# Attention plus MLP on one core: tails ahead of the main transposes, masks of batch 1 on VectorE, w_out sums one chunk later, casts ahead of loads

## The chip, the core and the metric

The kernel runs on one core of a Trainium2 chip. The core has TensorE (PE in the profile, with its weight loads as PEld), VectorE (DVE), ScalarE (ACT), GpSimd (POOL) and the queues that issue DMA transfers, of which SP and POOL matter here. The metric is the device time of one execution in microseconds (us).

## The reference

Input: q, k, v of 8 batches, 8 heads, 576 positions, 64 elements each; a two-layer MLP with w_in 512x2048, w_out 2048x512 and a slope alpha per hidden unit. All is float32 outside.

```python
scores = scale * np.matmul(q, k.transpose(0, 1, 3, 2))
mask_local = (rel >= 0) & (rel < 32)                  # heads 0 to 3
mask_strided = (rel >= 0) & (pos[None] % 32 == pos[:, None] % 32)   # heads 4 to 7
attn = softmax(np.where(masks, scores, -1e9))
x = (attn @ v), put as 4608 tokens x 512
h = x @ w_in
out = (np.maximum(h, 0) + alpha * np.minimum(h, 0)) @ w_out
```

Here rel is the query position less the key position.

## The kernel before

The work is in 16-bit floats with 32-bit sums. A batch has two **units** of four heads: the local heads (unit 2b) and the strided ones (unit 2b+1); a unit has two **pairs** of heads, so there are 32 pairs. For a unit, `transpose_piece` (L234) transposes q and then k on TensorE, eight 128x128 blocks each, into a PSUM tile `tp`, and copies them to SBUF (`qT`, `kT`). The rows 512 to 575 of q and k, loaded apart as a tile `tl`, are the **tails**: `tails` (L268) transposes them into a tile `tt`, and copies q's part on VectorE and k's part on ScalarE. For batches 0 and 1 (`early`) the two halves of each main copy are shared between VectorE and ScalarE (L256 to L262), and `tails` is called between k's two halves. One half of the copies waits for the other, since both read one PSUM tile. The tiles `tp`, `tt`, `pv`, `xp` and some scores share a ring of three PSUM banks (pool `ps`).

For a pair, scores are made in two groups (et tiles), exponentiated by ScalarE, and masked. Then `pv_piece` (L435) multiplies by v on TensorE (v has a column of ones, which gives the row sums), and VectorE takes the reciprocal (L458) and multiplies (L460). `x_piece` (L465) or a DMA transpose puts the result into `xT`.

There are three forms of masking. Batch 0 uses `score_piece` (L330), which adds a large negative mask (`madd`) to the scores by a matmul with the identity, ahead of the exponential. Batch 1 uses `score_early` (L290): it makes both score groups of a pair, adds the masks by four matmuls of 288 columns (L320), and then calls the exponentials (L323, L327). From batch 2 on, `score_both` (L388) masks after the exponential, by a multiplication with 0 or 1 on GpSimd (L423, L430).

The MLP goes over 9 chunks of 512 tokens. Layer 1 of a chunk is 16 `lin1_piece` (L623) of four matmuls; ScalarE makes the negative part (L643) and VectorE joins it (L646). Layer 2 of chunks 0 and 1 is 16 `lin2_piece` (L652) of four matmuls of 512 columns; from chunk 2 on, `lin2_sums` (L719) uses seven products of sums of blocks instead of eight products. It needs sums of blocks of w_out, which `w_sums` (L680) makes once: sums 1, 2 and 4 during layer 2 of chunk 0, and sum 3 in chunk 2.

The order is written out by hand: every instruction stays on its engine in program order (`keep`). Attention work is cut into pieces (L494 to L601), and `attn_step` (L611) runs the next piece between pieces of the MLP. The head (L864 to L882) runs batch 0's pieces with a few warming matmuls (`warm`) between them. Then come layer 1 of chunk 0 without attention pieces, and layer 2 of chunk 0 with batch 1's pieces, in the order that `alone(3, 2)` (L513) gives: q and k of the strided unit, scores of its two pairs, then pv pieces mixed with the transposes and scores of the local unit, and at last the x pieces. The first pieces of batch 2 follow.

GpSimd's queue carries loads that it issues itself and casts. Between L890 and L902 stand, in this order: the loads of batch 2's local q and k, two casts of batch 1's strided v (`cast_v`), the cast of batch 1's local q (`cast_l`), batch 2's tail loads, the cast of local k, a copy inside v (`over_v`), and more loads and casts for batch 2. The k and q casts feed the transposes of batch 1's local unit.

Of the kernel before, what the change touches and what calls it, by code (L numbers as in the profile page):

```python
# [11 lines left out]
ALU = mybir.AluOpType  # L12
AF = mybir.ActivationFunctionType
# [18 lines left out]
def kernel(  # L32
# [10 lines left out]
    nc = tc.nc  # L43
    keep = tc.keep_in_program_order
# [4 lines left out]
    SCALE = 1.0 / float(np.sqrt(D))  # L49
# [144 lines left out]
    def cast_v(b, pr, eng):  # L194

        v16 = vss[b % 2]
        cast_copy(eng, v16[0:72, 2 * pr : 2 * pr + 2, :, 0:64],
                  loaded[b][0:72, 1024 * pr : 1024 * pr + 1024].rearrange(
                      "p (h t d) -> p h t d", h=2, t=8))
        cast16[(b, True, "v")] = v16  # L200
# [33 lines left out]
    def transpose_piece(u, nm):  # L234

        b, strided = u // 2, u % 2 == 1  # L240
        early = b < NEARLY
        src = cast16[(b, strided, nm)]
        dst = qTs[u % 2][:, :, 0:576] if nm == "q" else kTs[u % 2][:, :, 32:608]
        tp = pspool.tile([128, 8, 64, 2], F16, tag="ps", name="tp")
        for j in range(8):
            blk = (src[:, j % 2, 128 * (j // 2) : 128 * (j // 2) + 128] if strided
                   else src[:, j].rearrange("p f d -> p (f d)"))
            keep(nc.tensor.transpose(tp[:, j].rearrange("r p e -> r (p e)"), blk, ident))  # L248
        if strided:
            main = tp.rearrange("r j p e -> r e j p")  # L250
            o = dst.rearrange("r e (j p) -> r e j p", j=8)[:, :, :, 0:64]
        else:
            main = tp.rearrange("r t p e -> r e p t")
            o = dst[:, :, 0:512].rearrange("r e (p t) -> r e p t", t=8)
        if early:
            for e in range(2):  # L256
                eng = "dve" if (nm == "q") == (e == 0) else "act"
                if u == 0 and nm == "q":
                    eng = "dve"
                if nm == "k" and e == 1:  # L260
                    tails(b, u, strided)
                cast_copy(eng, o[:, e : e + 1], main[:, e : e + 1])  # L262
            return
        cast_copy("act", o, main)
        if nm == "k":
            tails(b, u, strided)
# [23 lines left out]
    def score_early(P):  # L290

        w, r = P.w, 72 if P.strided else 128
        todo = []
        for i in range(2):
            et = ets[ectr["i"] % NE]
            ectr["i"] += 1
            if i:
                sps = [hbank() for _ in range(2)]
            else:
                sp = pbpool.tile([128, 2, 512], F32, tag="sp", name="sp")  # L300
                sps = [sp[:, y] for y in range(2)]
            grp = P.sgroups[i]
            n = w * len(grp)
            for x, t in enumerate(grp):
                k0 = 32 + 72 * t if P.strided else 96 * t
                for y in range(2):
                    hf = slice(64 * y, 64 * y + 64)
                    keep(nc.tensor.matmul(
                        sps[y][:, w * x : w * x + w], P.kT[hf, k0 : k0 + 128],
                        P.qT[hf, w * t : w * t + w], start=(x == 0), stop=False, skip_group_check=True))  # L310
                    P.et[(2 * (t // 2) + y, t % 2) if P.strided else (t, y)] = (et, n * y + w * x)
            todo.append((i, et[0:r, 0 : 2 * n], sps, n))
        for i, ev, sps, n in todo:
            if not P.strided and i == 0:
                m = madd[:, 0:288]
            else:
                m = madd[0:72, 288:360] if P.strided else madd[:, 96:192]
                m = m.unsqueeze(1).to_broadcast([r, n // w, w])
            for y in range(2):
                keep(nc.tensor.matmul(  # L320
                    sps[y][:, 0:n], ident[0:r, :], m, start=False, stop=True, skip_group_check=True))
            if i == 0:
                keep(nc.scalar.activation(  # L323
                    ev.rearrange("r (y c) -> r y c", y=2), sp[0:r, :, 0:n], AF.Exp, scale=SCALE))
                continue
            for y in range(2):
                keep(nc.scalar.activation(  # L327
                    ev[:, n * y : n * y + n], sps[y][0:r, 0:n], AF.Exp, scale=SCALE))

    def score_piece(P, i):  # L330

# [101 lines left out]
            defer.extend([lambda: ex(0), lambda: ex(1)])  # L433

    def pv_piece(P, a):  # L435
        while defer and any(P.et[z][0] is defer_et["et"] for z in P.et):
            defer.pop(0)()
        if P.x16 is None:
            if P.xd and P.strided:
                P.x16 = x16s  # L440
            else:
                P.x16 = xpool.tile([128, 1024], F16, tag="x16", name="x16")
        v16 = cast16[(P.b, P.strided, "v")]
        grp = P.pgroups[a]
        r = 72 if P.strided else 128
        pv = pspool.tile([128, 512], F32, tag="ps", name="pv")
        nb = 2 * len(grp)
        for x in range(nb):
            t, hh = grp[x // 2], x % 2
            et, c = P.et[(t, hh)]  # L450
            keep(nc.tensor.matmul(  # L451
                pv[:, 65 * x : 65 * x + 65], et[0:r, c : c + 128],
                v16[0:r, 2 * P.pr + hh, t, :] if P.strided else v16[:, 6 * (2 * P.pr + hh) + t, :],
                start=(x == 0), stop=(x == nb - 1), skip_group_check=True))
        w = P.w
        rc = rpool.tile([128, 8], F32, tag="rc", name="rc")
        pvv = pv[0:w, 0 : 65 * nb].rearrange("r (c e) -> r c e", e=65)
        keep(nc.vector.reciprocal(rc[0:w, 0:nb], pvv[:, :, 64]))  # L458
        c0 = 128 * grp[0]
        keep(nc.vector.tensor_tensor(  # L460
            P.x16[0:w, c0 : c0 + 64 * nb].rearrange("r (c e) -> r c e", e=64),
            pvv[:, :, 0:64],
            rc[0:w, 0:nb].unsqueeze(2).to_broadcast([w, nb, 64]), op=ALU.mult))
# [75 lines left out]
    for g in range(7, npair + 2):  # L539
        c = g // 4  # L540
# [68 lines left out]
    late = []  # L609

    def attn_step(end):  # L611
        if pos["i"] < end:
            pieces[pos["i"]][1]()
            pos["i"] += 1
        while late:
            late.pop(0)()
        if defer:
            defer.pop(0)()
# [188 lines left out]
    def warm(n):  # L807

        for _ in range(n):
            keep(nc.tensor.matmul(wps, wrm[:, 0:128], wrm, start=True, stop=True))  # L810
# [58 lines left out]
        madd, consts[:, 128:488], -1.0, 30000.0, op0=ALU.add, op1=ALU.mult))  # L869
    apt = pspool.tile([128, 512], F32, tag="ps", name="apt")  # L870
    for i in range(end0):
        if i == 9:
            keep(nc.tensor.transpose(apt[:, 0:16], alpha_r, id16))
            keep(nc.vector.tensor_scalar(
                oma, apt[:, 0:16], -1.0, 1.0, op0=ALU.mult, op1=ALU.add))
        if i == 8:
            cast_v(0, 0, "dve")
        attn_step(end0)
        if i < 2:
            warm(4)  # L880
        elif i > 8 and i not in (10, 13, 15):
            warm(1)  # L882

    def attn_n(n, end):
        for _ in range(n):
            attn_step(end)
        if n == 0:
            attn_step(0)

    load_qk(2, False, "q")  # L890
    load_qk(2, False, "k")
    for pr in range(2):
        cast_v(1, pr, "pool")
    cast_l(1, "q")
    load_tail(2, False)
    cast_l(1, "k")
    over_v(1, "pool")
    load_v(2, False)
    load_d(2)
# [8 lines left out]
        attn_n(0, end1)  # L908
    for i in range(16):
        lin2_piece(0, i)  # L910
        if i in (1, 3, 5):
            w_sums(nc.vector, ({1: 1, 3: 2, 5: 4}[i],))
        attn_n((0, 1, 1, 1, 1, 2, 1, 2, 1, 2, 1, 2, 2, 3, 2, 0)[i], end1)
        if i > 13:
            attn_n(1, end1 + 2)
# [5 lines left out]
    for n in range(1, NCH):  # L921
        ab = attn_until(n + 1) if n + 1 < B else len(pieces)
        left = ab - pos["i"]
        acc = 0.0
        for i in range(32 if n == 1 else 30):
            if i < 16:
                if n > 1:
                    lin1_piece(n, 8 * (i % 2) + i // 2)
                    if i in (5, 9, 13):
                        g_sum(nc.gpsimd, n, 1, i // 2 - 2, i // 2)  # L930
                else:
                    lin1_piece(n, i)
            elif n == 1:
                lin2_piece(n, i - 16)
            else:
                lin2_sums(n, i - 16)
                if n == 2 and i == 20:
                    w_sums(nc.vector, (3,))
            acc += left / (22.5 if n == 1 else 19 if n == B - 2 else 20.5) * (0.5 if i < 16 else 1.0)
            cnt = int(acc)  # L940
            acc -= cnt
            attn_n(cnt, ab)
        while pos["i"] < ab:
            attn_step(ab)
# [30 lines left out]
```

## Time and profile before

| | us |
|---|---|
| median of 6 runs | 311.62 (310.78 to 312.41) |
| the profiled execution | 311.78 |
| its span, first to last instruction | 310.0 |

| stage of the profiled execution | from | to | TensorE busy | VectorE busy | GpSimd busy |
|---|---|---|---|---|---|
| head: batch 0's attention | 0 | 23.0 | 23.00 | 15.99 | 18.41 |
| layer 1, chunk 0 | 23.0 | 38.5 | 15.38 | 12.23 | 4.16 |
| layer 1, chunk 1 | 62.6 | 78.7 | 16.06 | 12.30 | 9.23 |
| the rest, from chunk 2 on | 96.9 | 310.0 | 207.48 | 157.06 | 101.08 |

The two stages left out, layer 2 of chunks 0 and 1, are shown word for word in the prediction. The busy time of TensorE in the head has the warming matmuls in it. Times are from the start of the span. In a timeline a row has the start, the time, the engine, the line, the operation, the output and input tiles, the shape and a count; in square brackets stands the idle time ahead of it with what ended it. Rows of one engine may overlap by about 0.1 us. For a matmul the time includes the way through the array: four matmuls of 512 columns show 1.03 us, while the next matmul starts 0.86 us after the first. The granted TensorE clock was 0.999 of full speed.

### The profile page before, as it was taken

What the parts mean: (1) busy time and instruction counts of PE and PEld (TensorE: products, weight loads), DVE (VectorE), ACT (ScalarE), POOL (GpSimd) and SP (SyncE); (2) the same over time, 40 slices, a digit from 0 to 9 for tenths busy, and PEclk for the clock granted to TensorE, in tenths of its full rate; (3) what the DMA queues carried; (4) which work ended last, traced back from release to release, by engine and by line L of the source; (5) the groups of instructions that cost most, each with busy time, mean ns of one, the idle gap of its engine ahead of it and who ended that gap; (6) DMA issues with size and microseconds to landing.
All of it is one profiled execution on the core that took longest, in us unless ns stands there. A gap on an engine that the chain in (4) does not pass through costs nothing.

```text
span 310.0 us, 7066 instructions
## 1 busy us (share of the span) xinstructions
PE 300.3 (97%) x2803; PEld 192.5 (62%) x2803; DVE 219.2 (71%) x409; ACT 177.9 (57%) x330; POOL 170.0 (55%) x176
## 2 busy tenths in 40 slices
PE   8899989999999999999999999999999999999995
PEld 3554455654554468645888887448844784685484
DVE  6687875558533988488748874887579958855872
ACT  3656653597547764677467665766476336515630
POOL 8772399747979764967396719671825302201200
PEclk9999999999999999999999999999999999999999
DMA  7999999999899984999499819972911040012003
GB/s 233 195 207 206 213 205 199 174 170 257 145 172 220 154 102 38 152 271 128 61 174 261 100 30 181 142 82 37 190 53 22 2 123 34 2 51 87 0 3 135
DMA packets 81201, 40.38 MB, mean 130 GB/s; under 512 B 58624, under 2 KB 76304, under 8 KB 81168
## 3 DMA queue, kind: packets, MB, share of 16 engines
q0 software_dynamic: 41728, 17.38, 48.2%
q1 hardware_dynamic: 39168, 22.03, 32.3%
q10 hardware_dynamic: 272, 0.52, 0.5%
q8 instruction: 22, 0.36, 0.5%
q14 instruction: 11, 0.09, 0.1%
HBM read 38.01 MB, written 9.44 MB: 153 GB/s over the span
## 4 chain that ended last, share of the span: by engine, by line
PE 67%; DVE 12%; ACT 7%; POOL 4%; issue 4%; DMA 4%; SPq 0%; ACTq 0%; POOLq 0%; DVEq 0%
PE hb L633 27%; PE hb L752 20%; PE hb L660 6%; DVE gT L646 5%; DMA kl<-in_k_dram 4%; PE pv L451 3%; DVE x L460 2%; PE tp L248 2%; POOL vs L192 2%; ACT neg L643 2%; ACT et L421 2%; ACT xT L490 2%; PE sp L408 2%; ACT et L427 1%; PE xp L468 1%
## 5 line engine op out<-in xcount | busy, mean ns | idle before, releaser
L633 PE MATMUL hb<-xT,win 128*128 128x512 f16 (+1 forms) x640 | 132.9, 358 | 0.7
L646 DVE SCALAR_TENSOR_TENSOR gT<-neg,oma,hb 128x512 f16<-128x512 f32 x144 | 105.1, 744 | 38.3 <-ACT neg L643 31.9
L643 ACT ACTIVATE neg<-hb 128x512 f32<-128x512 f32 x144 | 86.0, 597 | 38.7 <-PE hb L633 37.3
L633 PEld LDWEIGHTS <-win 128*128 128x128 f16 x640 | 60.0, 98 | 56.6 <-issue 2.9
L423 POOL TENSOR_TENSOR et<-et,consts 128x576 f16<-128x576 f16 (+1 forms) x24 | 30.6, 1276 | 52.1 <-ACT et L421 52.1
L704 POOL TENSOR_TENSOR gsum<-gT 128x512 f16<-128x512 f16 x21 | 24.2, 1150 | 50.6 <-DVE gT L646 50.6
L752 PEld LDWEIGHTS <-gsum 128*128 128x128 f16 x448 | 41.3, 97 | 5.9 <-DVE gsum L704 1.1
L752 PEld LDWEIGHTS <-gT 128*128 128x128 f16 x336 | 31.4, 98 | 6.7 <-DVE gT L646 1.6
L460 DVE TENSOR_TENSOR x<-pv,rc 96x384 f16<-96x384 f32 (+2 forms) x62 | 33.0, 532 | 2.1
L660 PE MATMUL hb<-wout,gT 128*128 128x512 f16 x128 | 32.3, 379 | 0.0
L430 POOL TENSOR_TENSOR et<-et,consts 128x576 f16<-128x576 f16 (+1 forms) x24 | 30.6, 1277 | 0.6 <-ACT et L427 0.6
L764 ACT COPY o<-hb 128x512 f32<-128x512 f32 (+1 forms) x28 | 15.8, 565 | 26.4 <-PE hb L752 26.4
L451 PEld LDWEIGHTS <-et 72*128 72x128 f16 (+1 forms) x448 | 23.6, 98 | 9.6 <-DVE vs L190 0.4
L752 PE MATMUL hb<-wout,gT 128*128 128x256 f16 x216 | 28.0, 273 | 0.5
L458 DVE RECIPROCAL rc<-pv 72x6 f32<-72x6 f32 (+2 forms) x80 | 14.6, 183 | 19.5 <-PE pv L451 19.5
L752 PE MATMUL hb<-wout,gsum 128*128 128x256 f16 x216 | 26.9, 273 | 0.2 <-DVE gsum L704 0.2
L752 PE MATMUL hb<-wsum,gsum 128*128 128x256 f16 x216 | 26.3, 273 | 0.2 <-DVE gsum L704 0.2
L421 ACT ACTIVATE et<-sp 128x576 f16<-128x576 f32 (+1 forms) x24 | 15.5, 645 | 17.9 <-PE sp L408 17.9
L767 DVE TENSOR_TENSOR o<-hb,o 128x512 f32<-128x512 f32 (+1 forms) x21 | 14.2, 677 | 14.3 <-PE hb L752 10.6
L427 ACT ACTIVATE et<-sph 128x288 f16<-128x288 f32 (+1 forms) x48 | 18.2, 409 | 0.0
L192 POOL COPY vs<-stv 72x1024 f16<-72x1024 f16 x15 | 17.2, 1154 | 0.0
L660 PEld LDWEIGHTS <-gT 128*128 128x128 f16 x128 | 10.9, 97 | 9.0
(105 smaller groups left out, 324.2 us busy)
## 6 DMA issues: line engine op xcount, KB each, us to landing
out_dram<-o SPq DMA_DIRECT2D x27, 256.0 KB, 3.0
kl<-in_k_dram SPq DMA_DIRECT2D x6, 512.0 KB, 7.9
ql<-in_q_dram SPq DMA_DIRECT2D x5, 512.0 KB, 7.5
stv<-in_v_dram POOLq DMA_DIRECT2D x8, 288.0 KB, 7.5
vl<-in_v_dram POOLq DMA_DIRECT2D x6, 384.0 KB, 8.7
win<-in_moe_w_in_dram POOLq DMA_DIRECT2D x4, 512.0 KB, 11.7
wout<-in_moe_w_out_dram POOLq DMA_DIRECT2D x4, 512.0 KB, 14.2
out_dram<-osb SPq DMA_DIRECT2D x8, 256.0 KB, 5.6
```

The source lines that it names most:

```text
L192: keep(nc.gpsimd.tensor_copy(o, i))
L421: keep(nc.scalar.activation(ev.rearrange("r (y c) -> r y c", y=2), sp[0:r, :, 0:n], AF.Exp, scale=SCALE))
L423: keep(nc.gpsimd.tensor_tensor(mv, mv, m, op=ALU.mult))
L430: keep(nc.gpsimd.tensor_tensor(mv, mv, m, op=ALU.mult))
L451: keep(nc.tensor.matmul(pv[:, 65 * x : 65 * x + 65], et[0:r, c : c + 128], v16[0:r, 2 * P.pr + hh, t, :] if P.strided else v16[:, 6 * (2 * ...
L460: keep(nc.vector.tensor_tensor(P.x16[0:w, c0 : c0 + 64 * nb].rearrange("r (c e) -> r c e", e=64), pvv[:, :, 0:64], rc[0:w, 0:nb].unsqueeze ...
L633: keep(nc.tensor.matmul(hps[:, dst : dst + w], win16[:, kk, 128 * m : 128 * m + 128], xT[:, kk, src : src + w], start=(kk == 0 and x == 0) ...
L643: keep(nc.scalar.activation(neg, hps, AF.Relu, scale=-1.0))
L646: keep(nc.vector.scalar_tensor_tensor(gTs[n][:, m, :], neg, oma[:, m : m + 1], hps, op0=ALU.mult, op1=ALU.add))
L660: keep(nc.tensor.matmul(ops, gTs[n][:, kf, 128 * mt : 128 * mt + 128], wout16[:, kf, :], start=(kf == 0), stop=(kf == 15)))
L704: keep(eng.tensor_tensor(o[:, k0:k1], x[:, k0:k1], y[:, k0:k1], op=op))
L752: keep(nc.tensor.matmul(dst, lhs[:, kf, 128 * mt : 128 * mt + 128], rhs[:, kf, :], start=(first and own and kf == 0), stop=(kf == 7), skip ...
```

## The change

1. **Tails first.** For batches 0 and 1, `tails` is called ahead of k's main transposes, not between the two copies of k. So the `tt` bank is taken ahead of k's `tp` bank, and the small copies stand ahead of k's main copies on ScalarE and VectorE.
2. **Masks of batch 1 on VectorE.** `score_early` loses its 16 mask matmuls. After the exponentials it puts a multiplication of the et tile with the 0/1 mask on a list; `run_masks`, called at the start of each `attn_step` and each `pv_piece`, gives it to VectorE two steps later or when its pair's pv piece comes.
3. **w_out sums 1, 2 and 4** move from layer 2 of chunk 0 (after its pieces 1, 3 and 5) to layer 2 of chunk 1 (after its pieces 2, 6 and 10). They stay on VectorE.
4. **GpSimd's queue.** The four casts of batch 1 (v, q, v, k in this order) stand ahead of the loads of batch 2's q and k and of its tails.
5. In the head, the transpose of alpha and the scaling that reads it go from step 9 to step 3, and one warming matmul goes.

```diff
@@ transpose_piece
+        if early and nm == "k":
+            tails(b, u, strided)
         tp = pspool.tile([128, 8, 64, 2], F16, tag="ps", name="tp")
...
-                if nm == "k" and e == 1:
-                    tails(b, u, strided)
                 cast_copy(eng, o[:, e : e + 1], main[:, e : e + 1])
@@ score_early
-                        P.qT[hf, w * t : w * t + w], start=(x == 0), stop=False, skip_group_check=True))
+                        P.qT[hf, w * t : w * t + w], start=(x == 0), stop=(x == len(grp) - 1),
+                        skip_group_check=True))
...
-            for y in range(2):
-                keep(nc.tensor.matmul(
-                    sps[y][:, 0:n], ident[0:r, :], m, start=False, stop=True, skip_group_check=True))
...
+            if not P.strided and i == 0:
+                mv = ev.rearrange("r (y c) -> r y c", y=2)
+                m = mfirst.unsqueeze(1).to_broadcast([r, 2, n])
+            else:
+                mv = ev.rearrange("r (c f) -> r c f", f=w)
+                m = (mstr if P.strided else mother).unsqueeze(1).to_broadcast([r, 2 * n // w, w])
+            dmask.append([0, P, lambda mv=mv, m=m: keep(
+                nc.vector.tensor_tensor(mv, mv, m, op=ALU.mult))])
+
+    dmask = []
+
+    def run_masks(P=None):
+
+        for z in list(dmask):
+            z[0] += P is None
+            if z[0] > 1 or z[1] is P:
+                z[2]()
+                dmask.remove(z)
@@ pv_piece
+        run_masks(P)
@@ attn_step
+        run_masks()
@@ the head
-        if i == 9:
+        if i == 3:
             keep(nc.tensor.transpose(apt[:, 0:16], alpha_r, id16))
...
-            warm(4)
+            warm(4 - i)
@@ GpSimd's queue
+    cast_v(1, 0, "pool")
+    cast_l(1, "q")
+    cast_v(1, 1, "pool")
+    cast_l(1, "k")
     load_qk(2, False, "q")
     load_qk(2, False, "k")
-    for pr in range(2):
-        cast_v(1, pr, "pool")
-    cast_l(1, "q")
     load_tail(2, False)
-    cast_l(1, "k")
     over_v(1, "pool")
@@ layer 2 of chunk 0
-        if i in (1, 3, 5):
-            w_sums(nc.vector, ({1: 1, 3: 2, 5: 4}[i],))
@@ layer 2 of chunk 1
+                if i in (18, 22, 26):
+                    w_sums(nc.vector, ({18: 1, 22: 2, 26: 4}[i],))
```

More of the change, by code (lines that the diff above doesn't have):

```diff
@@ L313, in score_early @@
         for i, ev, sps, n in todo:
[L314 to L318, printed above, removed]
-            for y in range(2):
-                keep(nc.tensor.matmul(
-                    sps[y][:, 0:n], ident[0:r, :], m, start=False, stop=True, skip_group_check=True))
             if i == 0:
@@ L324, in score_early @@
                     ev.rearrange("r (y c) -> r y c", y=2), sp[0:r, :, 0:n], AF.Exp, scale=SCALE))
[L325 to L328, printed above, removed]
+            else:
+                for y in range(2):
+                    keep(nc.scalar.activation(
+                        ev[:, n * y : n * y + n], sps[y][0:r, 0:n], AF.Exp, scale=SCALE))
+            if not P.strided and i == 0:
+                mv = ev.rearrange("r (y c) -> r y c", y=2)
+                m = mfirst.unsqueeze(1).to_broadcast([r, 2, n])
+            else:
+                mv = ev.rearrange("r (c f) -> r c f", f=w)
[9 more added lines that the diff above has]
+                dmask.remove(z)
     def score_piece(P, i):
```

## The prediction

> **What bounds the kernel now.** I read the page's engine totals first, then a table of engine time by stage, then the chain of waits inside the one stage where TensorE stands still, and last the timelines of the instructions that the change touches.
>
> ```profile
> PE 300.3 (97%) x2803; PEld 192.5 (62%) x2803; DVE 219.2 (71%) x409; ACT 177.9 (57%) x330; POOL 170.0 (55%) x176
> ```
> ```profile
> 38.50:62.60 24.10, 22.66 (x271) 13.94 (x269) 14.62 (x31) 12.39 (x27) 20.97 (x22) 1.00 1.48 194
> 78.70:96.90 18.20, 18.04 (x174) 9.38 (x171) 7.02 (x19) 9.96 (x19) 16.13 (x17) 1.00 0.95 154
> ```
> TensorE (first busy column of the table) sets the end: it is busy 97% of the span and 18.04 of 18.20 us in layer 2 of chunk 1. The stage with a hole is layer 2 of chunk 0 (38.50 to 62.60), where it is busy 22.66 of 24.10 and GpSimd (fifth column) 20.97. So an edit counts where it takes matmuls away or closes that hole. The chain inside this stage:
>
> ```profile
> 38.33 1.22 DVE wsum L692
> ...
> 40.70 0.72 POOL ql L123
> ...
> 42.18 3.81 POOL vs L192 x2
> 45.99 0.99 POOL ql L192
> ...
> 47.03 0.62 PE tp L248 x8
> ```
> GpSimd issues batch 2's loads, makes two v casts and only then batch 1's q cast; the transposes of q on TensorE wait for it until 47.03 (1.21 us of TensorE idle in the waits). The v casts took 3.81 us for two, where one alone takes 1.03.
>
> ```profile
> 42.14 0.42 PE L320 MATMUL sp<-madd,consts 72*128 72x288 f16 x2
> 42.39 0.41 PE L320 MATMUL hb<-madd,consts 72*128 72x288 f16 x2
> 42.64 0.60 PE L660 MATMUL hb<-wout,gT 128*128 128x512 f16 x2
> ```
> The four mask matmuls of one score_early occupy TensorE from 42.14 to 42.64, 0.50 us. Two of VectorE's w_out sums (3.19 us from 41.90) run beside the slow casts.
>
> **The head, to 22.7 us: a loss.** Tails before the main transposes change the order on ScalarE. The rows of batch 0's second unit, ScalarE's and then VectorE's (start, us, engine, line):
>
> ```profile
> 12.56 0.57 ACT L188 COPY kT<-tp 128x512 f16<-128x512 f16 x1
> 13.03 0.27 ACT L188 COPY kT<-tt 128x128 f16<-128x128 f16 x1
> ```
> ```profile
> 12.63 0.21 DVE L190 COPY qT<-tt 128x128 f16<-128x128 f16 x1
> 13.16 0.69 DVE L190 COPY kT<-tp 128x512 f16<-128x512 f16 x1 [0.32 <-ACT kT L188]
> 13.77 0.48 DVE L190 COPY vs<-stv 72x1024 f16<-72x1024 f16 x1
> ```
> The first pv piece starts at 14.31, after 0.32 of waiting for that last copy. Today ScalarE's main copy of k starts at 12.56. In the new order it stands behind ScalarE's tail copy, which by the built program's waits needs VectorE's tail copy of q, and that stands behind two q copies. Steps: (1) batch 0's first unit: ScalarE has the same qT copy and kT copy, but both small tail copies ahead instead of one of them; the first scores start at about 9.84, not 9.70 (+0.14). (2) The alpha transpose now stands between the two score pieces; its row is 0.23, I take 0.15 since matmuls overlap. (3) q copies then end at 13.0 instead of 12.72, VectorE's tail copy at 13.12, ScalarE's tail copy at 13.42 and, with 0.1 overlap as in the rows, its main copy at 13.90 instead of 13.13. VectorE's second half, the v cast and the first pv follow: +0.77. From there VectorE runs reciprocal and multiply (0.19 and 0.55) ten times almost without a gap until 22.33, so nothing absorbs it. The sum is 0.77; it cannot be a gain, because no copy leaves this path, so the bounds are 0 and 1.0 (0.77 plus the rest of the 0.23). One warming matmul less (0.22) falls into an idle wait: nothing. The scaling that reads alpha (0.16 on VectorE) falls between its waits: nothing.
>
> **Layer 2 of chunk 0: the gain**, walked on before's clock. A layer-2 step is 0.86 on TensorE, a transposed unit 0.45.
> (a) No w_out sum stands ahead of the first q copy, and the tails come first: the first score_early starts at 41.60 instead of 41.77. Its masks go, 0.50. The second one must still wait for exponentials to free its banks, as now. Its masks go, 0.50.
> (b) On GpSimd the first v cast starts at 40.70, when the load issue ahead of it ends. Its data landed at 40.15 (issue 29.35 plus 10.8) and q's at 41.48. With nothing from VectorE beside them the casts take 1.03, 1.04, 1.03 and 1.07: q is ready at 42.8. TensorE comes to it at 44.50 and ends it at 44.95, now 47.48: **2.53 gained**, the hole included.
> (c) What is late next: the q copies of this unit. VectorE's queue is now reciprocal and multiply (to 45.47), two masks, q's first half (0.68), and then ScalarE's half (0.58), which frees the bank that the k transposes now use. (Before, the tails used it.) I price a mask by the same kind of instruction of nearly its size:
>
> ```profile
> 114.12 0.43 DVE L704 TENSOR_TENSOR gsum<-gT 128x512 f16<-128x512 f16 x1
> 114.47 1.29 DVE L704 TENSOR_TENSOR gsum<-gsum,gT 128x1024 f16<-128x1024 f16 x2
> ```
> 512 elements 0.43, 1024 elements 0.68 each: 576 elements 0.46, and 0.85 for a pair with their overlap. The bank is free at 47.55, TensorE is there at 46.97: 0.58 lost, gain 1.95. The bounds of a mask are 0.43 and 1.35 (the same 128x512 form at 240.96, beside GpSimd work); I take 0.46, since most masks meet GpSimd while it issues loads.
> (d) Two more score_early lose 0.50 each: 2.95.
> (e) At the end, masks of both last pairs (1.7 us) stand between reciprocals and multiplies; the last pv piece and the last x transposes wait about 0.4 together: **2.55**.
>
> Three edges of this. The last v copy of the unit still waits for its landing at 48.3, and ends a little earlier than now. Batch 2's q and k loads go out 4.2 us later (44.95 instead of 40.70); with 8.6 us they land at 53.6, their casts end by 56, and TensorE wants them from about 58. If that cover of 2 us went, each us more would count in full. The tail loads behind them only move with GpSimd's queue, the SP queue keeps its order, and transposed loads shift with TensorE.
>
> A row speaks on contention: beside two w_out sums (3.19) two v casts cost 1.75 more than 2 times 1.03. The Trainium skill, GPSIMD Engine Reference, Specifications, says that GpSimd's SBUF interfaces are shared with VectorE and contend with instructions that have two SBUF inputs. The masks are of that kind and the matmuls were not, so the rule speaks against this edit. By it each mask would hold GpSimd for its own length, eight by 0.46 or 3.7 us, the batch-2 casts would end near the 58 us where they are wanted, and up to 1 us of the gain would go; by the row beside load issues nothing goes.
>
> **W_out sums in chunk 1.** Three by 1.21 on VectorE, which is busy 7.02 of 18.20 us there and waits 0.21 to 1.75 before each reciprocal. They delay the reciprocal by 0 to 1.0 (by their places); the bank that it frees is wanted 2 us later. GpSimd loses up to 1.0 per sum (2.03 against 1.03) and has 2.07 idle; its masks are made about 2 us ahead of pv. I take nothing; the bounds are 0 and 1.73 each (1.94, the slower of the two sums shown, less the smallest wait of 0.21). It cannot gain: nothing leaves that stage.
>
> **Sum.** 0.77 minus 2.55 is -1.78. The profiled execution took 311.78 (span 310.0 and 1.8 around it), which gives 310.0; the median of the runs is 311.62, 0.16 lower, so 309.8.
>
> **Rivals.** *VectorE becomes the bound* in layer 2 of chunk 0. For it: a mask beside GpSimd can take 1.35, and masks stand ahead of copies that TensorE wants. Against: the VectorE time is no larger than the sums that leave (eight by 0.46, 3.7, against 4.41). At 0.9 per mask, between the two rows, the waits of (c) and (e) grow by some 0.9 each, the gain falls to about 0.8 and the head eats it: 311.5. *The head costs nothing*, if ScalarE's small copies fall into waits; against it are the dependencies above. Then 309.1. *Slower:* the w_out sums in chunk 1 hold the banks of pv and GpSimd's masks. For it: that stage has no hole on TensorE and GpSimd is 89% busy. Against: the waits of VectorE quoted. It decides once TensorE loses over 0.9 per sum (1.78 plus 0.93, by three); two of three at their bound of 1.73 cost 3.5: 313.3. *Not doing what it says*, q still late, is unlikely: its data landed at 41.48, three us before TensorE comes.
>
> **Numbers.** Forecast 0.48 (309.4 to 310.7 by itself: the head's upper bound, and masks up to 0.65 whose waits cost 0.4 twice), head free 0.17, VectorE bound 0.20, slower 0.15. 0.3% is 0.93 us, about what this measurement tells from none. So faster 0.65, same 0.20, slower 0.15. The range leaves out the slow case and reaches past the VectorE case and below the free head: 308.8 to 312.0.
>
> **What would show it.** Right: no mask matmuls, masks near 0.46 on VectorE; q's transposes at about 45.3 (44.5 plus the head) without a wait for GpSimd; the first layer-1 matmul near 23.5; chunk 1's first transposes at about 58.8 instead of 60.6; a TensorE wait for ScalarE's q copy before k's transposes. Wrong: first layer-1 matmul at 22.75 or before (head free), masks over 0.8, or TensorE waiting in 78 to 97.

## The result, and the profile after

The changed kernel took 310.29 us in the median of 25 runs; the kernel before took 311.57 in 53 runs beside it. The ratio, taken over the fast runs alone (one of the 25 was slow), is 0.9966 [0.9957, 0.9976], so the change makes the kernel faster by 0.34%. The forecast of 309.8 was 0.5 us too low; 310.29 lies inside the 309.4 to 310.7 that the prediction gave to its own mechanism. The profiled execution took 311.04 (span 309.2).

The totals of the page, and the two layer-2 stages of the table by stage (from:to, length, then busy time of PE, PEld, DVE, ACT, POOL, granted clock, DMA share, GB/s):

```profile
PE 297.7 (96%) x2786; PEld 190.9 (62%) x2786; DVE 222.9 (72%) x417; ACT 178.3 (58%) x330; POOL 169.7 (55%) x176
```
```profile
38.50:60.00 21.50, 20.00 (x241) 11.61 (x240) 15.34 (x38) 10.88 (x26) 19.19 (x22) 1.00 1.45 199
76.50:95.00 18.50, 18.33 (x177) 9.67 (x176) 11.79 (x25) 9.91 (x18) 15.47 (x15) 1.00 0.90 171
```

TensorE lost 2.6 us of work (297.7 against 300.3), yet the span shrank by 0.8. In layer 2 of chunk 0 there is still a hole: 20.00 busy of 21.50. Layer 2 of chunk 1 has none (18.33 of 18.50), with three w_out sums more on VectorE. The chain of waits shows who is late in layer 2 of chunk 0 now (start, time, piece):

```profile
46.70 0.73 DVE et L329 x2
47.44 0.61 DVE qT L190
...
48.07 0.59 ACT qT L188
...
54.99 1.76 DVE et L329 x2
...
57.58 0.56 DVE x L472
```

GpSimd is gone from the chain; q's transposes start at 45.72 and wait for nothing. In its place VectorE stands twice, with the new masks (L329): once ahead of q's copies, which free the bank that k's transposes need, and once at the end, ahead of the last pv pieces. A part of the timeline shows the wait of k's transposes, and why the last masks are long:

```profile
48.71 0.61 PE L250 MATMUL tp<-consts,kl 128*128 128x128 f16 x8 [0.35 <-ACT qT L188]
...
54.91 1.84 DVE L329 TENSOR_TENSOR et<-et,consts 128x576 f16<-128x576 f16 x2
55.18 1.26 POOL L192 CAST kl<-kl 128x1024 f16<-128x1024 f32 x1
...
57.49 0.34 PE L463 MATMUL pv<-vl,et 128*128 128x65 f16 x6 [0.55 <-DVE x L472]
...
58.19 0.36 PE L463 MATMUL pv<-vl,et 128*128 128x65 f16 x6 [0.35 <-DVE x L472]
```

Two such masks take 0.81 where nothing runs beside them (at 52.55, for one). The last two run beside GpSimd's cast of batch 2's k and take 1.84; TensorE then waits 0.55 and 0.35 us for VectorE.

The head lost time, as forecast: the first pv piece starts at 15.29 and not at 14.31. The timeline of batch 0's second unit:

```profile
11.97 1.29 DVE L190 COPY qT<-tp 128x512 f16<-128x512 f16 x2 [0.86 <-PE tp L250]
...
13.42 0.27 ACT L188 COPY kT<-tt 128x128 f16<-128x128 f16 x1 [0.22 <-DVE qT L190]
13.59 0.59 ACT L188 COPY kT<-tp 128x512 f16<-128x512 f16 x1
...
15.29 0.34 PE L463 MATMUL pv<-vs,et 72*128 72x65 f16 x6 [0.40 <-DVE vs L190]
```

ScalarE's tail copy stands ahead of its main copy of k and waits for VectorE's tail copy of q. That much is the mechanism of the prediction. But not all of the 0.98 is the change, as the second profile of the kernel before shows.

### The profile page after: what moved, and what is told of

The parts are those of the page before. It is cut to its first block, busy times and chain, and to the rows that moved or that the text cites. A ratio compares the mean times of both kernels' runs of the same rounds, so it can differ in the third digit from the quotient of the medians.

```text
span 309.2 us, 7042 instructions
## 1 busy us (share of the span) xinstructions
PE 297.7 (96%) x2786; PEld 190.9 (62%) x2786; DVE 222.9 (72%) x417; ACT 178.3 (58%) x330; POOL 169.7 (55%) x176
## 4 chain that ended last, share of the span: by engine, by line
PE 70%; DVE 14%; ACT 9%; issue 4%; DMA 2%; SPq 0%; ACTq 0%; DVEq 0%
PE hb L646 29%; PE hb L765 22%; PE hb L673 7%; DVE gT L659 5%; PE pv L463 3%; DVE x L472 3%; PE tp L250 2%; ACT xT L502 2%; DMA kl<-in_k_dram 2%; ACT neg L656 2%; PE sp L419 2%; ACT et L432 2%; ACT et L438 2%; PE xp L480 1%; PE opl L765 1%
```

## The experiments

The theory after the result: tails first and alpha cost the head what was forecast; the masks pay for it, less what they lose beside GpSimd's casts. Rivals: another part of the change brings the gain, or the head's loss was not the tails. Four marks of each trace are used below: the start of the **cast** of k at the head, the **first pv** piece, the first layer-2 matmul, and **chunk 1's transposes** (the first ones behind layer 2 of chunk 0). The time between the last two is called the **stage**. The last column has the four pairs of masks in their order. All times in us. A row with "before" or "changed" is one profiled execution.

| execution | time | cast of k | first pv | stage | mask pairs |
|---|---|---|---|---|---|
| before | 311.78 | 6.54 | 14.31 | 23.76 | |
| before, again | 310.99 | 6.85 | 14.59 | 22.61 | |
| changed | 311.04 | 6.87 | 15.29 | 21.97 | 1.72, 0.81, 0.81, 1.84 |
| changed, again | 310.25 | 6.94 | 15.43 | 21.15 | 1.64, 0.81, 0.81, 1.02 |

### The kernel before and the changed one, each profiled once more

No edit. Expected of the kernel before:

> The kernel before, unchanged, for one more profile. Theory: its first loads landed early by chance in the profile shown (cast of k at 6.54; 6.79 to 7.11 in every later profile), so here the cast of k starts at 6.8 to 7.1 and the first pv piece 7.8 us later. Rival: before's loads always land at 6.5, and the change costs the head that 0.3 too.

Measured: 310.99, span 309.1. The cast of k is at 6.85, and first pv 7.74 later. So the first loads of the profile that the prediction used had landed 0.3 early by chance. Counted from that cast, the first pv piece comes after 7.74 here, and after 8.42 and 8.49 in the two changed executions: the change costs the head 0.68 to 0.75. 0.77 had been forecast. The trace showed something else that had not been asked for, here in the timeline:

```profile
41.94 2.02 POOL L192 COPY vs<-stv 72x1024 f16<-72x1024 f16 x2
...
42.18 4.83 DVE L692 TENSOR_TENSOR wsum<-wout,wsum 128x2048 f16<-128x2048 f16 x2
...
43.91 2.03 POOL L192 CAST ql<-ql 128x1024 f16<-128x1024 f32 x1
...
45.99 0.62 PE L248 MATMUL tp<-consts,ql 128*128 128x128 f16 x8
```

The 1.21 us hole ahead of q's transposes is **not there**. In the first profile two v casts took 3.81 and the two w_out sums beside them 3.19; here the casts take 2.02 and the sums 4.83. The collision is the same, the other engine pays, and q is ready 0.05 us before TensorE comes (43.91 plus 2.03, against 45.99). The stage is 1.15 shorter for it. The hole is a matter of the execution, and the runs of the kernel before spread accordingly, nearly all between 310.6 and 312.4.

Expected of the changed kernel:

> The changed kernel itself, for a second profiled execution. In the first one the last pair of masks took 1.84 us beside GpSimd's cast of batch 2's k, on the chain, and that execution took 311.04 while the median is 310.29. My theory (the contention of VectorE and GpSimd falls on the chain in some executions only): if this execution takes 310.0 to 310.4, its last pair of masks takes 0.8 to 1.1 and chunk 1's first transposes start at about 59.0 instead of 59.76. Rival (the two levels come from the landing of the first loads): the last pair takes 1.8 as before, and the stages of the head start earlier by the difference.

Measured: 310.25, span 308.5. The last masks, on this timeline:

```profile
54.36 1.03 POOL L192 CAST kl<-kl 128x1024 f16<-128x1024 f32 x1
...
55.05 1.02 DVE L329 TENSOR_TENSOR et<-et,consts 128x576 f16<-128x576 f16 x2
```

The cast is nearly over when the masks begin; they take 1.02, not 1.84, and TensorE waits 0.2 in place of 0.9. This is what had been expected. The 0.7 us between the two changed executions (span 309.2 and 308.5) are these masks: 0.82 in the stage, less 0.14 by which this head was later.

### Tails as before

```diff
-        if early and nm == "k":
-            tails(b, u, strided)
         tp = pspool.tile([128, 8, 64, 2], F16, tag="ps", name="tp")
...
+                if nm == "k" and e == 1:
+                    tails(b, u, strided)
                 cast_copy(eng, o[:, e : e + 1], main[:, e : e + 1])
```

> The changed kernel with the tails again between the two copies of k, in both batches. My theory (the new order of the tails costs in the head because ScalarE's main copy of k waits for its tail copy): the first layer-1 matmul comes about 0.8 us earlier than in the changed kernel (22.9 to 23.1), and the median is 309.5 (309.2 to 309.8), against 310.3 of the changed kernel. Rival (the later head of the changed kernel is only the later landing of the first q and k loads in its profiled execution): the median stays at 310.3 within 0.2.

Measured: 309.86, ratio to the kernel before 0.9948 [0.9934, 0.9961]; 0.4 below the changed kernel, and just above the expected range. The intervals of the two overlap a little; the trace is clearer. From the second unit's first q copy to ScalarE's main copy of k it is 1.13 us, as in the kernel before; in the changed kernel 1.62. That is the 0.49 that this experiment was to find. The stage is 20.71, the shortest of all: TensorE no longer waits for ScalarE's q copy, and the last pair of masks takes 0.81. Of this the median shows only a part. In this execution 0.55 is lost again behind the stage, of it 0.39 in a wait for a transposed load of batch 2's k (`kT<-ksd`, at 72.33) that no other trace here has. How many of the runs have it is not known.

### Tails first in batch 1 only

```diff
-        if early and nm == "k":
+        if early and b == 1 and nm == "k":
             tails(b, u, strided)
...
+                if b == 0 and nm == "k" and e == 1:
+                    tails(b, u, strided)
```

> The changed kernel with the new order of the tails in batch 1 only. My theory: all of the loss sits in the head, so it equals the kernel with the old order in both batches within 0.2 us (309.5). Rival (the order also matters in layer 2 of chunk 0): the two differ by 0.3 us or more, to the better if the earlier k tails help the first scores, to the worse if the k transposes' wait for ScalarE's q copy is the price.

Measured: 310.17, 0.9958 [0.9942, 0.9974], 0.3 above the run before it. The head is as short as before (first pv 7.67 after the cast of k), but the stage is 21.5, with a wait of 0.35 of k's transposes for ScalarE's q copy. So the new order costs in batch 1 as well, as the rival said. The two stages can't be compared whole, since the masks differ too (the first pair 2.36 here, 1.84 with the old order; the last 1.02 and 0.81). Where the first pairs are alike, the new order puts the first scores of the local unit 0.33 to 0.39 later behind the first layer-2 matmul (12.44 against 12.11, and 12.80 against 12.41). The intervals of the two medians overlap; these marks decide, not the times.

### Alpha as before, and with it the tails

```diff
-        if i == 3:
+        if i == 9:
             keep(nc.tensor.transpose(apt[:, 0:16], alpha_r, id16))
...
-            warm(4 - i)
+            warm(4)
```

> The changed kernel with the alpha transpose at step 9 and all warming matmuls. My theory: the second scores of the head start 0.15 earlier and the median falls by 0.15, to 310.15 (310.0 to 310.3). Rival (it fell into a wait): the copies of batch 0's q start as late after the first scores as in the changed kernel (1.89 us), and nothing moves.

Measured: 310.13, 0.9959 [0.9943, 0.9975]. From the first scores to the second unit's q copy it is 1.73 again (changed 1.89): 0.16 shown, 0.15 forecast. The median moved as much, but that is less than these runs can tell.

The next run has both edits, the alpha one and the tails one. What is left of the change are the masks, the sums and GpSimd's order:

> The changed kernel without its two edits of the head: tails between the copies and alpha at step 9, all else changed. My theory: the head is that of the kernel before, so it is 0.15 below the kernel with the old tails alone: 309.7 (309.4 to 309.9), the fastest of all. Rival (the alpha edit is free): equal to the kernel with the old tails alone, 309.86.

Measured: 309.72, 0.9948 [0.9929, 0.9967]. It is the fastest version here, as expected: first pv 7.66 after the cast of k, as in the kernel before, and a stage of 21.0. It can't be told from the run with the tails alone. Two views of it show things that the runs above do not. Its first masks took 2.47, and now the transposes of the tails wait for ScalarE's q copy, in the old order:

```profile
PE tt L278 <- ACT qT L188: 0.3, 1, 0.3
```

And its last masks meet a cast and lose nothing; the cast pays:

```profile
54.06 1.85 POOL L192 CAST kl<-kl 128x1024 f16<-128x1024 f32 x1
```
```profile
54.20 0.81 DVE L329 TENSOR_TENSOR et<-et,consts 128x576 f16<-128x576 f16 x2
```

The same stands in the run with the old tails alone (cast of q 1.96, masks 0.81). So a part of the short stages of these two runs, 0.1 against a last pair of 1.02 and 0.9 against one of 1.84, comes from which engine paid, and not from the tails.

### Masks as before

```diff
-                        P.qT[hf, w * t : w * t + w], start=(x == 0), stop=(x == len(grp) - 1),
-                        skip_group_check=True))
+                        P.qT[hf, w * t : w * t + w], start=(x == 0), stop=False, skip_group_check=True))
...
+            for y in range(2):
+                keep(nc.tensor.matmul(
+                    sps[y][:, 0:n], ident[0:r, :], m, start=False, stop=True, skip_group_check=True))
...
-            dmask.append([0, P, lambda mv=mv, m=m: keep(
-                nc.vector.tensor_tensor(mv, mv, m, op=ALU.mult))])
...
-        run_masks(P)
...
-        run_masks()
```

> The changed kernel with batch 1's masks as matmuls again. My theory: 2.0 us of matmuls come back and TensorE's new waits on VectorE and ScalarE in layer 2 of chunk 0 (0.35 and 0.9) go, so it is 0.8 us slower than the changed kernel: 311.1 (310.8 to 311.4). Rival (VectorE is the bound of that stage, so the masks gained nothing): 310.3 or below.

Measured: 311.56, 1.0008 [0.9997, 1.002], with runs from 311.47 to 311.63 only. Everything but the masks brings nothing: the head's 0.7 eats what the sums and the queue give. The masks on VectorE are worth 1.3 us, of the 2.0 that their matmuls take on TensorE (four calls by 0.50). That is more than the 0.8 expected, which had taken the waits of the first changed execution (0.35 and 0.9); with those of the second (0.35 and 0.2) the same sum gives 1.4, an estimate.

This run has the tails first, and yet k's transposes do not wait for ScalarE's q copy. So that wait needs both parts of the change: with the old tails or without the masks on VectorE k's transposes do not have it.

### The order on GpSimd as before

```diff
-    cast_v(1, 0, "pool")
-    cast_l(1, "q")
-    cast_v(1, 1, "pool")
-    cast_l(1, "k")
     load_qk(2, False, "q")
     load_qk(2, False, "k")
+    for pr in range(2):
+        cast_v(1, pr, "pool")
+    cast_l(1, "q")
     load_tail(2, False)
+    cast_l(1, "k")
```

> The changed kernel with GpSimd's queue as before (loads of batch 2 ahead of the casts). My theory by the changed kernel's rows: without the w_out sums beside them the casts take 1.03 each, q is ready at about 45.4, TensorE comes at 45.7, so the order alone is worth nothing once the sums have moved: 310.3 within 0.2. Rival (the order itself is what closed the hole): the wait of 1.2 us returns, 311.5.

Measured: 311.01, 1.0001 [0.9981, 1.0022], between the two expectations. Neither mechanism: q's transposes wait for no cast. The first masks now meet both a v cast and the q cast. A row of the timeline, and the row of the waits that follows from it (waited for in total, times, longest):

```profile
44.00 2.71 DVE L329 TENSOR_TENSOR et<-et,consts 72x576 f16<-72x576 f16 x2 [0.37 <-ACT et L316]
```
```profile
PE tp L250 <- ACT qT L188: 1.0, 1, 1.0
```

They take 2.71 in place of 1.64, q's copies stand behind them, and k's transposes wait 1.03 instead of 0.35. The stage is 21.84 against 21.15, with equal last masks (1.02). So casts ahead of loads help by 0.7, but not through q: here they kept a cast away from the masks. That is read from one trace of each. With the new order the first masks took 1.50 to 1.84 in four traces, but 2.36 and 2.47 in two others, so the order does not rule this collision out.

### w_out sums as before

```diff
         lin2_piece(0, i)
+        if i in (1, 3, 5):
+            w_sums(nc.vector, ({1: 1, 3: 2, 5: 4}[i],))
...
-                if i in (18, 22, 26):
-                    w_sums(nc.vector, ({18: 1, 22: 2, 26: 4}[i],))
```

> The changed kernel with w_out sums 1, 2 and 4 in layer 2 of chunk 0 again. My theory (in that stage VectorE and GpSimd take each other's time, and the sums are the largest VectorE instructions there): the sums lengthen the casts to about 2.0 and the masks to over 1 us, q's copies come 1 us later, and the median is 311.3 (310.9 to 311.8). Rival (VectorE has room; only the wait for the q cast mattered, which the new queue order removes): 310.3 within 0.2.

Measured: 313.44, 1.0068 [1.0048, 1.0089]: slower than the kernel before, and far beyond what was expected. The timeline:

```profile
43.36 4.18 DVE L705 TENSOR_TENSOR wsum<-wout,wsum 128x2048 f16<-128x2048 f16 x2
43.43 2.05 POOL L192 COPY vs<-stv 72x1024 f16<-72x1024 f16 x1
...
47.97 0.51 PE L463 MATMUL pv<-vs,et 72*128 72x65 f16 x6 [2.27 <-DVE et L329]
...
49.22 2.07 DVE L329 TENSOR_TENSOR et<-et,consts 72x576 f16<-72x576 f16 x2
...
52.55 0.61 PE L250 MATMUL tp<-consts,kl 128*128 128x128 f16 x8 [0.20 <-ACT qT L188]
```

Two sums beside GpSimd's casts take 4.18, the masks stand behind them on VectorE, and the pv piece behind the masks: TensorE idles 2.27. Behind that hole the clock falls, in the table of stretches (columns as above, the clock third from the end):

```profile
46.00:48.00 2.00, 0.04 (x1) 0.04 (x2) 2.00 (x3) 0.00 (x0) 2.00 (x4) 0.97 0.52 82
48.00:50.00 2.00, 2.00 (x17) 1.45 (x18) 1.73 (x4) 0.00 (x0) 1.96 (x3) 0.50 0.76 279
```

By stretches of a quarter microsecond, half the clock was granted for 3.4 us, from 47.87 to 51.28 (the next expectation reads it as 3.6). At first sight that is 1.7 of the 3.15 us lost. The next run tests it.

### The same, with the hole filled

```diff
+        if P.b == 1 and P.strided and P.pr == 0 and a == 0:
+            for _ in range(9):
+                keep(nc.tensor.matmul(pv, wrm[:, 0:128], wrm, start=True, stop=True))
         for x in range(nb):
```

> The changed kernel with the w_out sums in layer 2 of chunk 0, as in the run sums_as_before, and with nine idle-work matmuls of 512 columns (zeros, into the bank that the first strided pv piece of batch 1 then overwrites) just ahead of that pv piece, where TensorE stood still for 2.27 us. They add nothing to the output. Theory: the loss of that run was the hole and, behind it, 3.6 us at half the granted clock (47.85 to 51.47), which is 1.8 us; with the hole filled (9 by 0.215 is 1.9 us) the clock stays at 1.0 and the time falls from 313.4 by about 1.5 to 1.8: 311.8 (311.4 to 312.1). Rival: the lower clock has another cause, or the stage waits for the masks in any case; then 313.2 to 313.6 with 0.5 still granted.

Measured: 313.49, 1.0056 [1.0036, 1.0076]: no gain at all, as the rival's second half had it. The clock did stay up, so the hole was its cause:

```profile
48.00:50.00 2.00, 1.85 (x25) 1.32 (x26) 1.88 (x6) 0.00 (x0) 1.96 (x4) 1.00 0.84 268
```
```profile
45.58 2.11 PE L462 MATMUL pv<-gsum 128*128 128x512 f16 x9
...
52.56 0.61 PE L250 MATMUL tp<-consts,kl 128*128 128x128 f16 x8 [1.58 <-ACT qT L188]
```

But k's transposes start at 52.56, and started at 52.55 at half clock. They wait for ScalarE's copy of q, which stands behind VectorE's first half, and that behind the contended masks (2.04). What TensorE gained by its clock it then waited (1.58). So the theory fell in its second half: the slow clock cost nothing here, because VectorE's queue of sums, masks and copies set the pace.

### The sums alone, and the queue alone

The kernel before with only the move of the w_out sums (the diff of "w_out sums as before", the other way round):

> The kernel before with only the move of the w_out sums to chunk 1. Theory: without sums beside them the two v casts take 2.1 instead of 3.8 us, q is cast 1.7 us earlier, the 1.21 us hole ahead of q's transposes closes, and chunk 1 loses nothing: 310.3 (310.0 to 310.6), ratio 0.996. Rival 1: the transposes then meet another wait as large (k's bank, or v): 311.0 to 311.6. Rival 2: the sums cost in chunk 1: over 311.6.

Measured: 310.72, 0.9979 [0.997, 0.9989], with all runs from 310.64 to 310.93. No hole: two v casts take 2.02 and the q cast 1.04, ready at 44.4. The rival of a next wait as large does not hold; but half a microsecond of the expected gain is missing, since the kernel before has the hole only in some executions. The narrow spread of the runs suggests what the move brings: none of them has it.

The kernel before with only the new order on GpSimd:

> The kernel before with only the new order on GpSimd (casts of batch 1 ahead of the loads of batch 2). The sums of w_out still run beside the casts. Theory: the q cast is second instead of fifth in the queue and ends by about 44, TensorE comes for it at 45.8, so the same 1.21 us hole closes: 310.4 (310.1 to 310.7), as much as the sums alone give, since there is one hole to close. Rival: the loads of batch 2 go out 4 us later and their transposes wait, or the casts still come late: 311.0 to 311.8.

Measured: 311.67, 1.003 [0.9999, 1.0061], with runs from 310.7 to 315.2: no gain that these runs can tell, against a forecast of 310.4. The profiled execution (310.7) has no hole, and its stage is 22.38, as with the sums alone (22.39). Why six of its twelve runs took over 312 is open; no trace of one was taken.

## Why the prediction was right, and where it was off

- **The head (0.77 lost): right**, 0.68 to 0.75 counted from the cast of k. Terms: first scores 0.04 to 0.11 later (0.14 forecast), alpha 0.16 (0.15), ScalarE's order 0.49 (0.48). The forecast mark of 23.5 for the first layer-1 matmul was 23.71; 0.33 of the difference to before is the landing of the loads. The rival of a free head is out.
- **Steps (a) and (d), the mask matmuls: right.** They are gone, and so are 17 matmuls with the warming one. In the changed kernel q's transposes start 7.93 behind the first layer-2 matmul, and 8.88 with the masks as matmuls. But the other half of (a) was wrong: the first scores were to start 0.17 earlier, and start 0.07 later (5.00 instead of 4.93 behind that matmul), since k's transposes now stand behind those of the tails (3.36 instead of 3.03; with the old order of the tails it is 4.93 and 3.03 again).
- **Step (b), 2.53 with the hole: the hole was taken for a constant.** It was in the profile but is not in every execution of the kernel before: 23.76 and 22.61 for the stage. Against the profile that the prediction read, the stage gained 1.79 and 2.61 (21.97 and 21.15; 2.55 forecast); against the execution without the hole, 0.64 and 1.46. The median of before holds runs of both kinds, so its gain had to be smaller than the sum.
- **Step (c), k's transposes waiting for ScalarE's q copy: right**, 0.35 instead of 0.58. It named both causes, the masks ahead of q's copies and the bank that the tails used before, and the runs show that both are needed. With the old order and long first masks the tails' transposes wait instead (0.3).
- **Step (e), and the price of a mask: mis-sized.** A pair was taken at 0.85. It takes 0.81 with no cast beside it, and also beside a cast where the cast pays; where VectorE pays, 0.88 to 2.71. The end was priced at 0.4 and took 0.9 in one execution, 0.2 in the other. The bound of 1.35 for one mask had been named, and set aside because "most masks meet GpSimd while it issues loads"; two pairs of four met casts in the first changed execution (0.86 and 0.92 for each mask, over the 0.8 that the prediction had named as a sign against it). So the rival in which VectorE becomes the bound came true in a part: TensorE waits for these masks, but loses less than it gains.
- **W_out sums in chunk 1 at nothing: right.** They take 1.22 to 1.35 each there in the first changed execution (up to 2.20 in the other traces), TensorE waits for none of them, and from chunk 1's transposes to the end it is 249.4 in all four executions of the table. What the prediction did not see is that the move is needed: with the masks on VectorE and the sums in their old place the kernel is slower than before (313.44). The slower rival had the right collision in the wrong stage.
- **The later loads of batch 2: the cover held.** In the first changed execution the cast of k ends at 56.44 and TensorE wants it at 61.07. No trace shows TensorE waiting for these casts.

The forecast in spans was 310.0 less 1.78, 308.2. Measured: 308.5 and 309.2. The first 0.3 is the landing; the other 0.7 is the last masks beside the cast of k. Chunk 1's first transposes, forecast at 58.8, were at 59.08 and 59.76, by the same two amounts. That the stage of the second execution fits so well (21.15, forecast 23.76 less 2.55, or 21.21) is in part luck: the first scores 0.24 later than forecast stand against waits that were 0.2 shorter in (c) and again in (e).

The rule that the prediction weighed (the Trainium skill, GPSIMD Engine Reference, Specifications: shared SBUF interfaces, contention with VectorE's two-input instructions) agrees with these traces in direction: masks and casts that overlap stretch. Pricing all masks by the rows beside load issues was the wrong choice for the pairs that met casts. But the loss that the prediction drew from the rule, GpSimd held up, was not what cost time here. Beside the last masks of the first changed execution the cast took 1.26 (alone 1.04) and the masks 1.84 (alone 0.81), and TensorE waited for the masks; where the cast paid (1.85 and 1.96, masks 0.81), TensorE waited for neither.

## What to carry to other kernels

Work moved from the busiest engine to one that is "only 72% busy" costs what its queue and its neighbour make of it: look at which instructions of GpSimd run in the same microseconds, price the pair, not the instruction, and move casts and sums out of the way in the same change. A hole that stands in one profile may be the accident of one execution; a second profile of the same kernel, or the spread of its runs, tells whether closing it is worth its length. And time lost by an engine counts only if the next thing it needs is already there: half the clock for 3.4 us cost nothing, because the copy it then waited for came no sooner.

## What the runs showed of the hardware

- Whole-tile instructions of VectorE and GpSimd that overlap can stretch either one: two v casts 3.81 and two sums 3.19 in one execution, 2.02 and 4.83 in another of the same kernel. Masks and casts do the same: 1.84 and 1.26 in one execution, 0.81 and 1.85 in another. What decides who pays was not found out.
- A hole of 2.27 us on TensorE was enough for half the granted clock over the next 3.4 us; with the hole filled by nine matmuls it stayed at 1.00. The Trainium skill (TensorE: Matmul & The Clock Gate, Part 1) puts the fall after about 3.4 us without work; here it came earlier, and the measurement decides. A gap of 1.58 a little later, in the filled run, left the clock at 1.00.
- The first loads of the head landed with a spread: the cast of k behind them started between 6.54 and 7.11 over all profiles, with nothing of it changed.
